# Spreading half of a block-diagonal table on the chip instead of loading it, with a new order of all work

## The chip, the cores and the metric

The kernel runs on one core of a Trainium2 chip. A core has five engines that run side by side, each with its own queue of instructions, worked off in order: PE (matrix products), DVE (vector work), ACT (activations, also copies with a scale), POOL (small vector work) and SP (here only issues DMAs). They meet through semaphores. On-chip data lies in SBUF (128 partitions) and, for PE's results, in eight banks of PSUM. The metric is the device time of one execution in microseconds.

## The reference

Two mixers, A and B, are applied twice in turn to x, of 2048 rows by 512 columns, each on a layer norm and with a residual:

```
x = A_q
x = x + A(layernorm(x));  x = x + B(layernorm(x))
x = x + A(layernorm(x));  x = x + B(layernorm(x))

A: k_shift = sum over 4 taps of shifted k * shift_k;   kv = k_shift * v
   y = irfft(rfft(kv, 4096) * rfft(ssm_k, 4096))[:2048]      (a causal long convolution per column)
   A = q * (y + kv * ssm_D)
B: gelu(layernorm(x) @ w1 + b1) @ w2 + b2                    (512 -> 1376 -> 512)
```

The convolution y does not depend on x, so it is computed once and used by both A layers. Its Fourier transforms are done as matrix products in two stages.

## The kernel before

All data lies in one SBUF tensor, `ar`, cut into named regions. The sequence is worked in two halves of 1024 positions. For the first half the steps are these; the names in brackets are used in the prediction, with the line that the profile gives.

- Loads, all issued by SP in 256 KB pieces: h (`ssm_k`, 4 pieces of a half: h0 to h3), k (k0 to k3), v (v0 to v3), and the second-stage table in 16 pieces (s0 to s15).
- T0 to T3: PE turns a block of h (L540), and DVE or ACT copies it from PSUM as 16-bit values (L473 on ACT, L474 on DVE).
- H1.0 to H1.7: first stage of the transform of h, 16 matmuls each (L557), evicted as 128x1024 (L473 or L474).
- H2.0 to H2.7: second stage (L569), 16 matmuls each. H2.t uses pieces 2t and 2t+1 of the table and all of H1. Eviction as before.
- swap: eight SBUF-to-SBUF DMAs that exchange even and odd partitions of H2's result. The first four need H2.0 to H2.3, the others H2.4 to H2.7.
- K0 to K3: PE turns a quarter of k (L589) and a copy follows. taps: PE turns the filter taps (L520), POOL forms diagonal tap matrices (L527). F0 to F3: the shift filter of a quarter as matmuls (L614). The v products: DVE multiplies a filter's PSUM result with v (L620). Each needs all four pieces of v.
- X1.0 to X1.7 and X2.0 to X2.7: the two stages for kv, with the same table (L557, L569).
- P0.0 to P7.1: sixteen products of the two spectra on DVE (L468, 128x1024). They need X2, H2 and the swapped H2.
- U0 to U3 and G1.0 to G1.7: turn and first stage for the second half of h.
- I1.0 to I1.7 (L674) and I2 (L696): the two stages back. I1.0 to I1.3 need all P with second index 0, the others all P.

Then come the layers: blocks of 128 to 512 rows; for a block statistics on DVE (L810, L811) and POOL (L815, L817, L825), normalisation on DVE (L836) or ACT (L835), product with y and residual (L468), a second statistics and normalisation, a turn (PE, L887, or a DMA), m1 (L899) with gelu on ACT (L904), m2 (L933) with the residual on DVE (L937). The second half's convolution is woven between the blocks.

The order is written out as three constant lists: `SEQ` lists the operations' numbers in the order in which they go to the queues, `ENGS` chooses the engine (a ACT, v DVE, p POOL) for each operation that may run on several, and `BANKS` gives the first PSUM bank of each PSUM tile. `arrange()` reads these, and `sync()` puts in the waits that data and banks demand. The durations in the code are the planner's; nothing waits by them.

The second-stage table holds, for each of 128 small matrices (128 columns each), a weight of 128 x 128 that is zero except where the partition's remainder by 8 equals the group of 16 columns: 7 of 8 values are zero. It is 4 MB in HBM, loaded whole.

Of the kernel before, what the change touches and what calls it, by code (L numbers as in the profile page):

```python
# [7 lines left out]
ALU = mybir.AluOpType  # L8
# [28 lines left out]
class Prog:  # L37
# [65 lines left out]
            "aavvvvvaavvvvvvv")  # L103
    BANKS = (
            "45704306202464200000627236026646246464226006402420624644066042640262264600644466440666002624266260062444"
            "46206466216237643301320727321504123101100322332716373063445423545175402012133355426403067156573421254373"
            "47061653171314250227620662421047670120016563423216502311505064403200454166210125364")

    def __init__(self, nc):
# [283 lines left out]
def bass_interleave_layers__ssm_conv_h3__mixer_channel_mlp__prompt_kernel(  # L393
        nc, A_q, A_k, A_v, A_shift_k, A_ssm_k, A_ssm_D, B_x, B_w1, B_b1, B_w2, B_b2, out):
    P = Prog(nc)
    ar = nc.alloc_sbuf_tensor("ar", [128, AR], BF16)
    NS = 352
# [576 lines left out]
```

## Time and profile before

| | us |
|---|---|
| median of 3 runs | 237.92 |
| lowest, highest | 237.78, 238.18 |
| the profiled execution | 237.62 |
| its span | 235.8 |

| engine | busy us | share of the span |
|---|---|---|
| PE matmul | 223.4 | 95% |
| PE weight load | 146.6 | 62% |
| DVE | 177.0 | 75% |
| ACT | 161.7 | 69% |
| POOL | 55.2 | 23% |

The profile is one execution. Its span goes from the first to the last instruction; 1.8 us of the execution's time lie around it. The shares are means over stages that differ much: the DMA engines move 304 GB/s from 5 to 10 us and 393 GB/s from 15 to 20 us, and 2 GB/s from 90 to 100 us. In the timelines a row that stands for several instructions has their count behind an x; in brackets stands how long the engine had been idle before it and what ended that.

### The profile page before, as it was taken

Reading aid. Unit: us, or ns where it says so; the run is one execution under the profiler, and the core shown is the slowest. Engines: PE = TensorE matmul, PEld = TensorE weight load, DVE = VectorE, ACT = ScalarE, POOL = GpSimd, SP = SyncE. Lnnn points to the kernel's source line nnn. Section 1 sums busy time; section 2 is a strip of 40 time slices with the busy share of each in tenths; the row PEclk is TensorE's granted clock in tenths of the full one; section 3 lists DMA queues with packets and bytes.
Section 4 is the critical chain, followed back from the end, with each engine's and each line's share of the span. In section 5 each row is a group of like instructions: output and inputs, shape, how many; then the busy total and the mean of one; then the engine's idle time right before and its main releaser. Section 6 shows DMA issues by size and latency. Waiting matters only on the chain.

```text
span 235.8 us, 6520 instructions
## 1 busy us (share of the span) xinstructions
PE 223.4 (95%) x2765; PEld 146.6 (62%) x2765; DVE 177.0 (75%) x355; ACT 161.7 (69%) x259; POOL 55.2 (23%) x117
## 2 busy tenths in 40 slices
PE   6796887998999999999999999999999999999995
PEld 3785777875968588667967585644444444444453
DVE  0678989999999999989999899385379388705004
ACT  2962999998996789998987995998037403810910
POOL 1550020924222405344002831402020301100000
PEclk9999999999999999999999999999999999999999
DMA  6999879983976930022140203301300140071302
GB/s 210 301 375 386 311 208 282 264 288 70 174 119 177 198 79 0 3 48 45 31 151 6 45 3 69 67 0 22 67 0 4 22 111 0 0 134 47 133 0 92
DMA packets 41113, 26.77 MB, mean 114 GB/s; under 512 B 23702, under 2 KB 33788, under 8 KB 41084
## 3 DMA queue, kind: packets, MB, share of 16 engines
q1 hardware_dynamic: 40786, 26.20, 41.2%
q8 instruction: 22, 0.36, 0.7%
q10 hardware_dynamic: 298, 0.16, 0.3%
q14 instruction: 7, 0.06, 0.1%
HBM read 15.07 MB, written 2.10 MB: 73 GB/s over the span
## 4 chain that ended last, share of the span: by engine, by line
PE 77%; DVE 7%; ACT 6%; SPq 4%; DMA 4%; issue 1%; DVEq 0%
PE ps L899 33%; PE ps L933 32%; ACT ar L473 6%; PE ps L569 4%; DMA ar<-in_A_v_dram 4%; DVE ar L468 4%; SPq L453 3%; PE ps L674 2%; PE ps L696 2%; DVE ar L620 2%; PE ps L557 2%; DVE ar L474 2%; PE ps L922 1%; PE ps L642 1%; SPq L463 0%
## 5 line engine op out<-in xcount | busy, mean ns | idle before, releaser
L904 ACT ACTIVATE ar<-ps,sm 128x256 bf16<-128x256 f32 (+4 forms) x143 | 64.8, 525 | 35.1 <-PE ps L899 34.8
L473 ACT ACTIVATE ar<-ps 128x1024 bf16<-128x1024 f32 (+3 forms) x77 | 71.6, 1003 | 14.7 <-PE ps L557 6.2
L899 PE MATMUL ps<-ar 128*128 128x256 bf16 (+4 forms) x572 | 81.0, 297 | 0.2 <-ACT ar L473 0.2
L933 PE MATMUL ps<-ar 128*128 128x512 bf16 (+1 forms) x341 | 78.3, 379 | 0.0
L899 PEld LDWEIGHTS ps<-ar 128*128 128x128 bf16 (+1 forms) x572 | 52.7, 100 | 26.1 <-ACT ar L473 0.3
L468 DVE TENSOR_TENSOR ar<-ar 128x512 bf16<-128x512 bf16 (+3 forms) x105 | 62.6, 641 | 4.5 <-ACT ar L473 3.0
L933 PEld LDWEIGHTS ps<-ar 128*128 128x128 bf16 (+1 forms) x341 | 32.5, 98 | 36.5 <-ACT ar L904 0.4
L810 DVE BATCH_NORM_STATS2 sm<-ar 128x6 f32<-128x512 bf16 x64 | 42.6, 682 | 0.4
L835 ACT ACTIVATE ar<-ar,sm 128x512 bf16<-128x512 bf16 x38 | 30.2, 823 | 12.6 <-DVE sm L822 10.5
L815 POOL TENSOR_SCALAR sm<-sm 128x2 f32<-128x2 f32 (+2 forms) x22 | 7.6, 347 | 109.0 <-DVE sm L811 108.4
L937 DVE TENSOR_TENSOR ar<-ar,ps 128x512 bf16<-128x512 bf16 x31 | 20.4, 679 | 16.1 <-PE ps L933 16.1
L817 POOL TENSOR_TENSOR sm<-sm 128x2 f32<-128x2 f32 (+2 forms) x26 | 21.2, 814 | 21.8 <-DVE sm L815 19.9
L557 PE MATMUL ps<-ar 128*64 128x128 bf16 x512 | 17.2, 221 | 2.8 <-POOL ar L468 1.2
L569 PE MATMUL ps<-ar 128*128 128x64 bf16 x512 | 18.3, 193 | 1.3 <-ACT ar L473 0.9
L569 PEld LDWEIGHTS ps<-ar 128*128 128x128 bf16 x512 | 16.9, 98 | 3.2 <-ACT ar L473 1.4
L557 PEld LDWEIGHTS ps<-ar 128*64 128x64 bf16 x512 | 14.8, 110 | 5.6 <-ACT ar L473 1.6
L474 DVE CAST ar<-ps 128x1024 bf16<-128x1024 f32 x13 | 15.8, 1220 | 2.4 <-PE ps L569 1.3
L836 DVE TENSOR_SCALAR ar<-ar,sm 128x512 bf16<-128x512 bf16 x26 | 9.9, 406 | 5.1 <-POOL sm L825 5.0
L825 POOL TENSOR_SCALAR sm<-sm 128x1 f32<-128x1 f32 x40 | 13.2, 347 | 1.9
L674 PE MATMUL ps<-ar 64*128 64x64 bf16 (+1 forms) x384 | 12.6, 203 | 0.5 <-ACT ar L473 0.3
L674 PEld LDWEIGHTS ps<-ar 64*128 64x128 bf16 (+1 forms) x384 | 11.9, 114 | 1.9 <-ACT ar L473 1.2
L767 DVE SCALAR_TENSOR_TENSOR ar<-ar,sm,ps 128x512 bf16<-128x512 bf16 x16 | 10.9, 744 | 0.4 <-PE ps L569 0.4
(42 smaller groups left out, 90.3 us busy)
## 6 DMA issues: line engine op xcount, KB each, us to landing
ar<-tab_s SPq DMA_DIRECT2D x16, 256.0 KB, 9.0
ar<-ar SPq DMA_DIRECT2D x16, 256.0 KB, 4.5
ar<-in_A_ssm_k_dram SPq DMA_DIRECT2D x8, 256.0 KB, 7.1
ar<-in_A_q_dram SPq DMA_DIRECT2D x8, 256.0 KB, 4.9
ar<-in_A_v_dram SPq DMA_DIRECT2D x8, 256.0 KB, 6.8
out_dram<-ar SPq DMA_DIRECT2D x7, 256.0 KB, 2.5
ar<-in_B_w_dram SPq DMA_DIRECT2D x4, 344.0 KB, 5.6
ar<-in_B_w_dram SPq DMA_DIRECT2D x5, 256.0 KB, 4.1
```

The costliest lines, as they stand in the source:

```text
L468: return P.op(eng, lambda e: e.tensor_tensor(o, a, b, op), dur, reads=[a, b] + list(more), writes=[o])
L473: return e.activation(dst, src(), AF.Copy)
L474: return e.tensor_copy(dst, src())
L557: r = e.matmul(Q(tl, 64 * ri, 64, i * 128, [1, 128]), w, m, start=True, stop=True)
L569: r = e.matmul(Q(tl, 0, 128, i // 8 * 512 + i % 8 * 4, [32, 16], [1, 4]), w, m, start=True, stop=True)
L674: r = e.matmul(Q(tl, 0, 128, i, *([32, 16], [1, 4]) if split else ([1, 128],)), w, m, start=n == 0, stop=n == 1)
L810: P.op(DVE, lambda e, sj=sj, x=x: e.bn_stats(sj, x), 600.0, reads=[x], writes=[sj])
L817: P.op(POOL, lambda e: e.tensor_tensor(r, v, hf, ALU.pow), 420.0 + 149.0 * n, reads=[v, hf], writes=[r])
L835: return e.activation(o, x, AF.Identity, bias=u, scale=r)
L899: r = e.matmul(Q(tl, 0, rows, 0, [1, w]), a, m, start=dk == 0, stop=dk == 3)
L904: P.op(ACT, lambda e, dst=dst, tl=tl, rows=rows, bias=bias, w=w: e.activation(dst, Q(tl, 0, rows, 0, [1, w]), AF.Gelu_apprx_tanh, bias=bia ...
L933: r = e.matmul(Q(tl, 0, 128, 0, [1, 512]), ins[fc][0], ins[fc][1], start=fc == 0, stop=fc == 10)
```

## The change

The table in HBM has two parts now: C, 128 x 2048, with the values and no zeros, and the whole one behind it. Of C the first 1024 columns are loaded into the region of w1 (`R_C`, 256 KB), which stands for the first half of the whole table. The second half, pieces s8 to s15, is loaded whole as before. Pieces s0 to s7 are not loaded. In their place eight operations "spread" (SP0 to SP7) write the first half: SPd copies all 64 groups of 16 values of C to column group d of 64 matrices, multiplied per partition with a mask that is 1 where the partition's remainder by 8 is d, and 0 elsewhere. So each writes 128 x 1024 values in runs of 16, and each of H2.0 to H2.3 and X2.0 to X2.3 needs all eight. On DVE a spread is a `tensor_scalar`, on ACT an activation with a scale. One small copy makes the masks (on POOL, after the small table's load).

All three lists of the order are new. What stands where on the queues for the first part, in the order of the queue (loads of 256 KB unless marked; other small work left out or named by its kind):

```
SP before:  h2 h0 h1 h3 q0 k1 k3 k2 k0 q1 v2 q2 v0 (bias) v1 s12 s4 v3 s3 (small) s7 s6 s1 s5 s8 s13 s2 s0 hh1
            s11 s10 hh3 s15 s9 s14 hh2 hh0 | swaps 0 1 2 3 4 5 7 6 | rest of q, w1, w2, T2
SP after:   h3 h1 h0 k3 k0 k1 k2 C h2 q0 v2 v3 v1 v0 s11 s8 s15 hh2 q3 hh3 s14 (small) q1 (bias) hh0 s9 s13 s10
            w1 q2 s12 hh1 (bias) | swaps 0 1 3 2, one piece of w2, swaps 5 4 6 7 | rest of w1, w2, T2
DVE before: taps d0 T3 2 statistics H1.3 . . H1.6 . H1.2 K0 K2 K1 . V3 V1 V2 V0 X1.2 3 statistics X1.5 H2.1 X1.0
            statistic . X1.3 . H2.7 . X2.1 U3 P1.0 P0.0 U0 P2.0 P3.0 P0.1 P7.0 P6.0 P4.0 P5.0 P5.1 P6.1 P3.1 P7.1
            P2.1 P4.1 P1.1
DVE after:  T1 T0 H1.3 K1 SP0 SP4 taps 2 statistics K2 SP2 K3 . . V2 SP5 V0 . V1 SP3 V3 SP6 X1.0 . statistic X1.3 . .
            X1.4 statistic . . H2.1 statistic U0 . H2.7 statistic H2.4 P0.0 P3.0 X2.2 U3 P1.1 P2.0 P2.1 P1.0 P6.0
            P4.0 P5.0 P7.0 P7.1 P0.1 P6.1 P5.1 P3.1 P4.1
ACT after:  loads, T3 H1.7 H1.6 H1.0 H1.1 K0 SP1 T2 H1.2 H1.5 H1.4 SP7 (norm) X1.2 U2 H2.3 H2.2 X1.6 H2.0 X1.1 X1.7
            X1.5 H2.5 X2.3 X2.0 H2.6 X2.6 X2.1 G1.1 X2.4 X2.7 X2.5 ...
PE after:   warm T3 T1 T0 H1.7 H1.3 H1.6 H1.0 H1.1 K1 K0 H1.2 taps T2 K2 K3 F0 F2 H1.5 H1.4 F1 F3 X1.0 X1.2 U2 X1.6
            H2.3 H2.2 X1.3 X1.4 H2.0 X1.1 X1.7 H2.1 X1.5 U0 H2.5 H2.7 X2.3 X2.0 H2.4 H2.6 ...
```

(V0 to V3 are the v products, hh the second half of h, d0 an addition of one row, a point a small operation of up to 0.2 us.) In the new order H1.4 uses the PSUM banks of V2's filter, so its matmuls wait on PE for V2. The normalisation ahead of the first block's turn is on ACT before and on DVE after. The shift taps' load stands behind ACT's table load instead of ahead of it.

The diff, with the number lists cut:

```diff
     SEQ = (
-        42, 0, 6, 43, 214, 1, 4, 33, 2, 5, 34, 41, 7, 3, 195, 9, 11, 10, 8, 196, 51, 14, 197, 45, 52, 12, 209, 46, 35,
...
+        0, 46, 8, 45, 35, 2, 6, 3, 5, 36, 12, 9, 1, 10, 11, 25, 4, 44, 217, 7, 56, 197, 15, 50, 16, 57, 14, 13, 47,
...
     ENGS = (
-            "avapapvpaavvaavaavaaaaavvvvapvppvavvavaavaavvaaaaaaaavaaaaaaaaavaavaaaaaapvpvaaaaaaaaaaaaaaaaaaaaaaaaaaa"
...
+            "pvavvvvvavpvpapapaaavaaaaavaavaavavavvvppvvvaavvaaavaavvaaaaaaaaavaaaaavaaaavaaaaaaapppvaaaaaaaaaaaaaaaaaa"
...
     BANKS = (
-            "45704306202464200000627236026646246464226006402420624644066042640262264600644466440666002624266260062444"
...
+            "26624320240260660466027405640260464422140204626240406006442460424046462002242440224402622420604066466004"
...
@@ -358,13 +358,18 @@
-    S2 = np.zeros((2, 8, 8, 128, 2, 8, 8))
-    for d in range(8):
-        S2[0, :, d, :, 0, :, d] = c
-        S2[1, :, d, :, 0, :, d] = s
-        S2[0, :, d, :, 1, :, d] = -s
-        S2[1, :, d, :, 1, :, d] = c
-    S2 = S2.transpose(0, 1, 2, 3, 6, 5, 4).reshape(128, 128 * 128)
+    S2 = np.zeros((2, 8, 8, 128, 8, 2))
+    S2[0, :, :, :, :, 0] = c[:, None]
+    S2[1, :, :, :, :, 0] = s[:, None]
+    S2[0, :, :, :, :, 1] = -s[:, None]
+    S2[1, :, :, :, :, 1] = c[:, None]
+    C2 = S2.reshape(128, 2048)
+    S2 = np.zeros((128, 128, 8, 16))
+    pd = list(range(8))
+    for j in range(8):
+        m = np.arange(128) % 8 == pd[j]
+        S2[m, :, j] = C2.reshape(128, 128, 16)[m]
+    S2 = np.concatenate([C2, S2.reshape(128, 16384)], 1)
@@ -383,6 +388,7 @@
     sg = np.where(np.arange(128)[:, None] % 2 == 0, -1.0, 1.0) * np.ones((1, 16))
+    sg[:, 8:] = np.arange(128)[:, None] % 8 == np.arange(8)
@@ -441,9 +447,10 @@
+    R_C = R_W1
-    M_B1, M_ST, M_MV, M_RS, M_HF, M_NM, M_SG = 0, 16, 208, 240, 256, 260, 276
-    assert M_SG + 1 <= NS
+    M_B1, M_ST, M_MV, M_RS, M_HF, M_NM, M_SG, M_MK = 0, 16, 208, 240, 256, 260, 276, 284
+    assert M_MK + 8 <= NS
@@ -494,11 +501,25 @@
+    tload(t_s2, 18432, 0, R_C, 1024)
     load_h(0, R_1)
     load_t(A_k, 0, R_8, 2)
     load_t(A_v, 0, R_8 + 4096, 2)
-    for i in range(16):
-        tload(t_s2, 128 * 128, i * 1024, R_S2 + i * 1024, 1024)
+    for i in range(8, 16):
+        tload(t_s2, 18432, 2048 + i * 1024, R_S2 + i * 1024, 1024)
+    P.tag = "spread"
+    mk, src = M(0, 128, M_MK, [1, 8]), A(0, 128, R_SG + 8, [1, 8])
+    P.op((DVE, POOL), lambda e, mk=mk, src=src: e.tensor_copy(mk, src), {DVE: 65.0, POOL: 190.0}, reads=[src], writes=[mk])
+    for h in range(1):
+        for d in range(8):
+            o, c, m = A(0, 128, R_S2 + 8192 * h + 16 * d, [128, 64], [1, 16]), A(0, 128, R_C + 1024 * h, [16, 64], [1, 16]), M(0, 128, M_MK + d, [1, 1])
+
+            def f(e, o=o, c=c, m=m):
+                if e is nc.scalar:
+                    return e.activation(o, c, AF.Copy, scale=m)
+                return e.tensor_scalar(o, c, m, None, ALU.mult)
+            P.op(BOTH, f, {ACT: 912.0, DVE: 395.0}, reads=[c, m], writes=[o])
+    P.tag = ""
     tload(t_sm, row, 464, R_U, 256)
```

More of the change, by code (lines that the diff above doesn't have):

```diff
@@ L44 @@
     SEQ = (
[55 rows of a table removed]
[55 rows of a table added]
     ENGS = (
-            "avapapvpaavvaavaavaaaaavvvvapvppvavvavaavaavvaaaaaaaavaaaaaaaaavaavaaaaaapvpvaaaaaaaaaaaaaaaaaaaaaaaaaaa"
-            "aappappaavpvppaappvvppaapvaappaappaapvaappaappavppvappaappaappvvppaappvappaaavvvvvaappvaaapvvvavpvvvavpp"
-            "aavvvvvaavvvvvvv")
+            "pvavvvvvavpvpapapaaavaaaaavaavaavavvvppvvvaavvaaavaavvaaaaaaaaavaaaaavaaaavaaaaaaapppvaaaaaaaaaaaaaaaaaa"
+            "aaaaaaaaaaapvapvvavpvppaappvvppaavpaappaappaappaappaappaappavppaappaavpvvppavppaapvaavavvvaaapvvavvvpaav"
+            "vpvvvvavvavvvvvavavpvvvaa")
     BANKS = (
-            "45704306202464200000627236026646246464226006402420624644066042640262264600644466440666002624266260062444"
-            "46206466216237643301320727321504123101100322332716373063445423545175402012133355426403067156573421254373"
-            "47061653171314250227620662421047670120016563423216502311505064403200454166210125364")
+            "26624320240260660466027405640260464422140204626240406006442460424046462002242440224402622420604066466004"
+            "64437020665061071760610567714342477554774645676076415011601640607710627426534031026021423236345773476356"
+            "05721367332244501304047053300705405345357130760457666515312732321600130735714203533")
     def __init__(self, nc):
```

108 rows, old and new, of the table SEQ are left out of this document.

## The prediction

> **What bounds the kernel now.** I read the page first, then busy time by stretches of the span, then the chain that ended last, then the timelines of DVE, ACT and SP over the first 60 us. Times below are microseconds from the span's start. The first fence has the page's lines of the span and of the engines, and then the stretches (per engine: busy time and instructions; then the clock, DMA share and GB/s).
>
> ```profile
> span 235.8 us, 6520 instructions
> ```
>
> ```profile
> 0.00:42.66 42.66, 34.02 (x787) 28.92 (x788) 30.80 (x45) 30.65 (x33) 10.06 (x31) 1.00 0.91 294
> 42.66:58.02 15.36, 14.37 (x240) 11.53 (x241) 14.49 (x32) 14.66 (x17) 7.29 (x11) 1.00 0.74 213
> 58.02:235.80 177.78, 175.06 (x1738) 106.17 (x1738) 131.68 (x280) 116.40 (x210) 37.87 (x77) 1.00 0.28 62
> ```
>
> From 58.02 on PE is idle for 2.7 us of 177.8, and most of that is the tail after its last matmul. There an earlier arrival of anything wins nothing; the end is where PE's saturated stretch begins, plus its work. What can be won lies before 58: 8.6 us of idle PE up to 42.66 and 1.0 after it. The chain says what holds PE there (start, length, what):
>
> ```profile
> 4.57 1.21 SPq L453
> ...
> 10.05 8.55 DMA ar<-in_A_v_dram
> ...
> 23.47 0.65 PE ps L569 x16
> ...
> 40.45 6.12 DVE ar L468 x10
> ...
> 57.28 0.70 ACT ar L835
> 58.02 0.41 PE ps L887 x4
> 59.11 0.84 PE ps L899 x12
> ...
> 233.45 0.29 DVE ar L926
> ```
>
> The last load of v, issued at 10.05, lands at 18.60; the four v products follow on DVE, then evictions and the spectrum products until 46.57 (40.45 + 6.12). The DVE timeline gives the durations (start, length, group; idle before it in brackets):
>
> ```profile
> 18.68 4.74 DVE L620 TENSOR_TENSOR ar<-ps,ar 128x1024 bf16<-128x1024 f32 x4 [2.09 <-DMA ar<-in_A_v_dram]
> 23.33 1.22 DVE L474 CAST ar<-ps 128x1024 bf16<-128x1024 f32 x1
> 24.46 1.87 DVE L810 BATCH_NORM_STATS2 sm<-ar 128x6 f32<-128x512 bf16 x3
> 27.75 2.36 DVE L474 CAST ar<-ps 128x1024 bf16<-128x1024 f32 x2 [0.29 <-PE ps L569]
> 32.55 1.23 DVE L474 CAST ar<-ps 128x1024 bf16<-128x1024 f32 x1 [0.39 <-PE ps L569]
> 34.51 1.23 DVE L474 CAST ar<-ps 128x1024 bf16<-128x1024 f32 x1 [0.66 <-PE ps L569]
> 35.65 0.68 DVE L474 COPY ar<-ps 128x1024 bf16<-128x1024 bf16 x1
> 38.05 8.51 DVE L468 TENSOR_TENSOR ar<-ar 128x1024 bf16<-128x1024 bf16 x14
> ```
>
> Neighbours overlap a little, so by steps a v product is 1.18, an eviction 1.16, a statistic 0.62, a 16-bit copy from PSUM 0.60 and a spectrum product 0.61. DVE's idle in this stretch is 0.29 + 0.39 + 0.66 = 1.34 us: from 18.68 on, DVE is the bound, and ACT beside it nearly so. What v's lateness costs is 2.09 us of idle DVE.
>
> **The loads.** Seven loads of 256 KB fewer go out, and the order on SP changes: the last load of v is the 14th large load instead of the 17th, the small table C the 8th. The SP timeline, with the landings of the same loads (us from issue) after it:
>
> ```profile
> 8.51 0.36 SPq L453 DMA_DIRECT2D ar<-in_A_v_dram  x1
> 10.05 0.50 SPq L453 DMA_DIRECT2D ar<-in_A_v_dram  x1
> 29.76 2.52 SPq L453 DMA_DIRECT2D ar<-ar  x2
> ```
>
> ```profile
> ar<-in_A_k_dram SPq DMA_DIRECT2D x2, 256.0 KB, 6.8
> ar<-in_A_v_dram SPq DMA_DIRECT2D x1, 256.0 KB, 8.1
> ar<-in_A_v_dram SPq DMA_DIRECT2D x1, 256.0 KB, 8.5
> ar<-ar SPq DMA_DIRECT2D x2, 256.0 KB, 4.7
> ```
>
> The 14th large load landed at 8.51 + 8.1 = 16.6, the 17th at 18.6. v is complete at 16.6, 2.0 us earlier. k moves up to the 4th to 7th place, h's block 2 down to the 9th; the 9th was issued at 4.57 and landed 6.8 later, at 11.4, the 8th a little before, so C is there near 11 (estimate from these rows). The table's whole half is spread over the 15th to 31st places, between q and the second half of h; its first user in stage 2 comes after H2.1's eviction (29.5, below), and an equal place landed several us before that, so it costs nothing; were that cover gone, PE would wait load by load, 0.65 us each (2.0 / 3). The loads of W1, W2 and the biases that now stand before or among the swaps have users from 59.11 on; one load of W2 between the swaps delays the later swaps by one issue, whose first product, P6.0, stands seventh. shift_k's load goes behind ACT's table load, while its user, the taps, moves back on PE behind K0 and H1.2.
>
> **The spreads.** No spread is in the trace. The nearest rows (line, operation, forms, count, busy, mean ns):
>
> ```profile
> L836 DVE TENSOR_SCALAR ar<-ar,sm 128x512 bf16<-128x512 bf16 x3 | 1.2, 402 | 0.0
> L468 DVE TENSOR_TENSOR ar<-ar 128x1024 bf16<-128x1024 bf16 x16 | 9.8, 691 | 0.0
> L811 DVE BATCH_NORM_AGGREGATE sm<-sm 128x2 f32<-128x6 f32 x10 | 1.4, 167 | 0.0
> L473 ACT ACTIVATE ar<-ps 128x1024 bf16<-128x1024 f32 x38 | 36.3, 1045 | 7.0 <-PE ps L557 5.9 <-PE ps L674 0.5 <-PE ps L569 0.3
> ```
>
> The same operation on half the elements is 0.40 (0.33 as a step, less the 0.07 to 0.08 by which neighbours overlap (0.691 against 0.61)), so that is the lower end; a product of two tensors of the same size is 0.69 (0.61 as a step), the upper. The operation is L836's, so I lean to it: 0.47, the middle of the steps, six times on DVE. On ACT a spread is at most the 1.0 of an eviction. [...]
>
> Spreads 0, 4 and 2 lie on DVE before the first v product. From C's arrival and the K1 copy before them, 11.6 (11 + 0.6), stand three spreads (1.41), the taps' copy (0.2), two statistics (1.24), two copies (1.20) and two small ones (0.34): done by 16.0, before v's 16.6, so they cost nothing; the cover is 0.6 us. The two on ACT fall into this row's gap:
>
> ```profile
> 21.62 1.02 ACT L473 ACTIVATE ar<-ps 128x1024 bf16<-128x1024 f32 x1 [4.79 <-PE ps L557]
> ```
>
> Spreads 5, 3 and 6 stand between the v products, on the path. Before, products to first eviction took 23.33 - 18.68 = 4.65. Now it is 4.65 + 3 x 0.47 + 0.15 for a small operation moved in from POOL = 6.2, so from 16.65 the first X1 eviction starts at 22.85: of 2.0 us, 0.5 is left. H2.3, the first second-stage group, needs all eight spreads and starts near 22.9 to 23.1, against 23.47. PE's queue has one new tie: H1.4 waits for the bank that the first v product frees (17.8), and filter F1 stands behind it; a stage group and a filter need some 1.6 us, and DVE comes to F1's product at 19.6, so it costs nothing with 0.2 to spare.
>
> **From there to the end of the spectrum products.** Both orders hold seven evictions, four statistics, two copies and sixteen products on DVE; the new one holds 0.48 more of small ones (a halo copy, an aggregate, a two-scalar step). Before: 46.57 - 23.33 = 23.24, less its 1.34 of waits, 21.9; after 22.4, to 45.2 without waits. But the swap loads wait for H2.1's eviction, which DVE now ends at 22.85 + 4 x 1.16 + 2 x 0.62 + 0.81 = 29.5, against 28.9 (27.75 + 1.16). The second swap moves from 29.76 to 30.4 and lands 4.7 later, at 35.1. The first product P0.0 could go at 45.2 - 16 x 0.61 - 1.16 - 0.60 = 33.7. It waits 1.4 us, everything behind it on DVE as well, and the products end at 46.6, against 46.57: zero. So the load that was late is paid back, and the next late thing is the swap. Bounds: -1.4 if the swaps land earlier on the emptier queue, +0.7 if spreads take 0.69.
>
> **The hand-over to the block.** Before, ACT evicts until 57.28, then normalises (0.70), PE turns (0.41), ACT copies, and the first m1 matmul is at 59.11. The new order puts that normalisation on DVE. DVE reaches it near 56.7 by its list (statistics and products of the first block from 52.8, then POOL's two steps, 0.9 together), so ACT no longer stands in line. This takes up to 0.7 from the chain. PE's idle there, 0.99, is the most that can go. I take -0.6; bounds 0 and -1.0.
>
> **The saturated stretch and the tail.** A fresh order cannot win there (2.7 us idle, of it 235.8 - 233.45 = 2.35 behind the last matmul) and can open new holes: 0 to +1.2, about as many as the stretch before 58 has. I take +0.2. The last four matmul groups are reordered, with the same pieces: zero. ACT, with as many evictions in both orders, gains what DVE gains.
>
> **Sum.** 0 - 0.6 + 0.2 = -0.4. The profiled execution took 237.62 us, so 237.2; the median of the runs is 0.30 above it, which gives 237.5.
>
> [...] POOL's two copies under DVE's run of products show a lock; the second line is the same size of copy when DVE was on other work (min/median/max ns):
>
> ```profile
> L632 POOL COPY ar<-ar x2: 199/2638/5077, 41.5 to 46.7; 128x3 bf16<-128x3 bf16 x2
> ```
>
> ```profile
> L603 POOL COPY ar<-ar x3: 189/190/191, 15.0 to 16.1; 128x3 bf16<-128x3 bf16 x3
> ```
>
> One copy took 5.08 us instead of 0.19. [...]
>
> **Rivals.**
> Slow spreads (slower): place, between the v products; price, 0.69 each and a wait on POOL, so the first X1 eviction at 23.5 to 24, the swaps at 30.3 to 30.7, and the products' end 0.7 to 1.3 later: 238.2 to 238.8. For it: it stores runs of 16 elements, a shape that no TENSOR_SCALAR row has. Against it: L836. It decides from 0.64 us a spread, where 3 x 0.17 eats the 0.5 that is left. Chance 0.28; the lock is 0.08 of it.
> The new order leaves holes in the saturated stretch (slower): 1.0 to 2.0 above the sum, 238.5 to 239.5. For it: nothing there can improve. Against it: PE's queue there holds blocks with two engines at 75% or less. Chance 0.14.
> The gain passes through (faster): spreads at 0.33 and no wait for the swaps, -0.4 - 1.4 on top of the sum: 235.7; half of it, 236.6. For it: seven loads less are queued ahead of the swaps. Against it: the swaps stood behind the last of the other loads before, too. Chance 0.20.
> My forecast, 237.0 to 238.0: chance 0.38.
>
> **How the numbers follow.** A run of this kernel tells 0.2% (0.48 us) from no change: faster is under 237.44, slower over 238.40. The forecast's 0.38 splits 0.20 faster, 0.18 same; the passing gain is faster, 0.20; slow spreads 0.03 same and 0.25 slower; holes 0.14 slower. Together 0.40, 0.21, 0.39. The range goes from half to nearly all of the passing gain, 235.9, to the worst of the holes, 239.5. The likeliest case alone has 237.0 to 238.0.
>
> **What would show it.** DVE's bracket before L620 gone or small, with its first row near 16.6; three TENSOR_SCALAR of 128x1024 between L620 rows, of 0.4 to 0.55; the first L569 near 23; the swaps' first issue near 29.6, and DVE idle before L468 with a DMA as releaser; the last L468 near 46.6; L835 gone from the chain at 57. Wrong it would be if L620 began before 16 or after 17.5, if L468 did not wait, or if PE idled more than 3.5 us behind 58.

## The result

| | before | changed |
|---|---|---|
| median us | 237.78 (22 runs) | 236.59 (22 runs) |
| lowest, highest | 237.21, 240.32 | 235.99, 240.65 |
| ratio, 95% interval | | 0.9955 [0.9935, 0.9975] |
| the profiled execution's span | 235.8 | 237.0 |

The change wins 0.45%. In two later comparisons the same kernel gave 0.9988 [0.9958, 1.0019] and 0.9941 [0.991, 0.9971], so the gain lies between nothing and 0.6%, most likely near 0.4%. Executions of the changed kernel are spread more than its gain is wide, and the profiled one is 2.2 us above its median (238.78). In some comparisons a part of the executions had a mean granted clock of 0.993 or less and was some 1.6 us longer (6 of 35 of the kernel before beside e9 to e12, with a median of 239.5 against 237.9; 4 of 12 in e5; 7 of 10 in e3; none of 12 in e9), so medians of different comparisons differ by that as well. So the traces below are read for mechanisms, and the sizes are compared over several of them.

The profile of the changed kernel. First the page's line of the span, then the busy time in the stretches used before (columns as before):

```profile
span 237.0 us, 6515 instructions
```

```profile
0.00:42.66 42.66, 35.65 (x814) 30.00 (x815) 33.27 (x54) 35.05 (x38) 11.27 (x34) 1.00 0.86 274
42.66:58.02 15.36, 14.76 (x252) 11.92 (x250) 14.96 (x33) 14.49 (x21) 3.78 (x9) 1.00 0.67 167
58.02:237.00 178.98, 173.74 (x1710) 104.10 (x1706) 130.84 (x278) 116.26 (x208) 34.91 (x68) 1.00 0.26 60
```

Up to 58 us PE did 2.0 us more work than before (35.65 + 14.76 against 34.02 + 14.37). Behind 58 it is idle for 5.2 us of its span, against 2.7 before: the front got faster, and the saturated stretch got holes. The DVE timeline shows the front:

```profile
13.79 0.68 DVE L520 TENSOR_SCALAR ar<-ar,sm 128x1024 bf16<-128x1024 bf16 x1
15.33 1.23 DVE L641 TENSOR_TENSOR ar<-ps,ar 128x1024 bf16<-128x1024 f32 x1
16.47 0.48 DVE L520 TENSOR_SCALAR ar<-ar,sm 128x1024 bf16<-128x1024 bf16 x1
16.86 1.22 DVE L641 TENSOR_TENSOR ar<-ps,ar 128x1024 bf16<-128x1024 f32 x1
21.34 1.22 DVE L481 CAST ar<-ps 128x1024 bf16<-128x1024 f32 x1
32.81 1.28 DVE L475 TENSOR_TENSOR ar<-ar 128x1024 bf16<-128x1024 bf16 x2
36.20 8.52 DVE L475 TENSOR_TENSOR ar<-ar 128x1024 bf16<-128x1024 bf16 x14 [0.37 <-issue]
```

The first v product (now L641) starts at 15.33 with no wait; before, L620 waited until 18.68. Spreads are L520. The first X1 eviction is at 21.34 (23.33 before), and the products end at 36.20 + 8.52 = 44.72 (46.57). The loads behind this, in the SP timeline and the times to landing (the last load of v, the second swap):

```profile
7.72 0.46 SPq L460 DMA_DIRECT2D ar<-in_A_v_dram  x1
...
28.77 2.77 SPq L460 DMA_DIRECT2D ar<-ar  x4
```

```profile
ar<-in_A_v_dram SPq DMA_DIRECT2D x1, 256.0 KB, 7.3
ar<-ar SPq DMA_DIRECT2D x1, 256.0 KB, 2.9
```

v is complete at 7.72 + 7.3 = 15.0. The second swap, issued at 29.52, lands at 32.4, ahead of the first product. The chain that ended last, from the hand-over on, and PE's two waits on it:

```profile
55.21 0.41 PE ps L908 x4
...
56.30 0.84 PE ps L920 x12
...
66.84 4.29 DMA ar<-ar
71.19 4.55 PE ps L920 x40
...
79.31 4.88 DMA ar<-ar
84.25 7.60 PE ps L920 x68
```

```profile
71.19 4.98 PE L920 MATMUL ps<-ar 128*128 128x256 bf16 x44 [1.06 <-DMA ar<-ar]
84.25 5.96 PE L920 MATMUL ps<-ar 128*128 128x256 bf16 x53 [1.61 <-DMA ar<-ar]
```

The normalisation on ACT is gone from the hand-over, and the first m1 matmul is at 56.30 instead of 59.11. But PE then waits 1.06 and 1.61 us for the DMA transposes (L900) that bring the normalised rows of blocks 2 and 3 to m1. Before, m1 had no such wait:

```profile
72.29 4.98 PE L899 MATMUL ps<-ar 128*128 128x256 bf16 x44
83.58 9.33 PE L899 MATMUL ps<-ar 128*128 128x256 bf16 x84
```

That is the second half of the story: 2.7 us which the prediction had as 0.2.

### The profile page after: what moved, and what is told of

Read it like the earlier page. It is cut to its first block, busy times and chain, and to the rows that moved or that the text cites. A ratio compares the mean times of both kernels' runs of the same rounds, so it can differ in the third digit from the quotient of the medians.

```text
span 237.0 us, 6515 instructions
## 1 busy us (share of the span) xinstructions
PE 224.1 (95%) x2765; PEld 146.0 (62%) x2765; DVE 179.1 (76%) x363; ACT 165.8 (70%) x263; POOL 50.0 (21%) x110
## 4 chain that ended last, share of the span: by engine, by line
PE 75%; ACT 8%; DMA 8%; DVE 5%; SPq 1%; issue 1%
PE ps L920 32%; PE ps L954 28%; DMA ar<-ar 6%; ACT ar L480 6%; PE ps L695 4%; PE ps L590 3%; PE ps L578 3%; DMA ar<-in_A_ssm_k_dram 2%; ACT ar L856 2%; DVE ar L475 2%; DVE ar L641 2%; PE ps L717 1%; DVE ar L481 1%; PE ps L635 1%; SPq L460 1%
## 5 line engine op out<-in xcount | busy, mean ns | idle before, releaser
L925 ACT ACTIVATE ar<-ps,sm 128x256 bf16<-128x256 f32 (+4 forms) x143 | 66.1, 521 | 37.2 <-PE ps L920 36.8
L954 PE MATMUL ps<-ar 128*128 128x512 bf16 (+1 forms) x341 | 79.6, 379 | 0.0
L475 DVE TENSOR_TENSOR ar<-ar 128x512 bf16<-128x512 bf16 (+2 forms) x104 | 62.9, 642 | 5.9 <-ACT ar L856 4.4
L954 PEld LDWEIGHTS ps<-ar 128*128 128x128 bf16 (+1 forms) x341 | 32.3, 98 | 35.1 <-ACT ar L925 0.2
L856 ACT ACTIVATE ar<-ar,sm 128x512 bf16<-128x512 bf16 x39 | 30.7, 811 | 10.2 <-DVE sm L843 10.2
L838 POOL TENSOR_TENSOR sm<-sm 128x2 f32<-128x2 f32 (+2 forms) x26 | 21.4, 824 | 41.4 <-DVE sm L836 39.8
L836 POOL TENSOR_SCALAR sm<-sm 128x2 f32<-128x2 f32 (+2 forms) x19 | 5.9, 310 | 92.0 <-DVE sm L832 91.8
L578 PE MATMUL ps<-ar 128*64 128x128 bf16 x512 | 18.3, 221 | 1.9 <-ACT ar L480 1.2
L481 DVE CAST ar<-ps 128x1024 bf16<-128x1024 f32 x11 | 13.4, 1216 | 1.5 <-PE ps L578 1.2
L832 DVE BATCH_NORM_AGGREGATE sm<-sm 128x2 f32<-128x6 f32 x64 | 10.5, 173 | 0.8
```

What stands on the lines that cost most here:

```text
L475: return P.op(eng, lambda e: e.tensor_tensor(o, a, b, op), dur, reads=[a, b] + list(more), writes=[o])
L578: r = e.matmul(Q(tl, 64 * ri, 64, i * 128, [1, 128]), w, m, start=True, stop=True)
L838: P.op(POOL, lambda e: e.tensor_tensor(r, v, hf, ALU.pow), 420.0 + 149.0 * n, reads=[v, hf], writes=[r])
L856: return e.activation(o, x, AF.Identity, bias=u, scale=r)
L925: P.op(ACT, lambda e, dst=dst, tl=tl, rows=rows, bias=bias, w=w: e.activation(dst, Q(tl, 0, rows, 0, [1, w]), AF.Gelu_apprx_tanh, bias=bia ...
L954: r = e.matmul(Q(tl, 0, 128, 0, [1, 512]), ins[fc][0], ins[fc][1], start=fc == 0, stop=fc == 10)
```

## The experiments

The theories. **A, the place:** v's place in the queue of loads sets the front; the smaller table and the spreads are not what wins. **B, the bytes:** the front wins because seven loads of 256 KB less go out. **C, swap traffic:** the waits near 71 and 84 come from the second half's swaps on the same DMAs. **D, instruction packets,** formed after C fell: a 16 KB packet of the queue that loads instructions holds one DMA engine while a transfer needs a part from that engine. Several edits move operations in `SEQ` with this helper:

```diff
+def _put(seq, ids, after):
+    s = [i for i in seq if i not in ids]
+    k = s.index(after) + 1
+    return tuple(s[:k]) + tuple(ids) + tuple(s[k:])
```

All runs in one table. "Products" is the end of the last spectrum product, "m1" the start of the first m1 matmul, "rest" the span less that, "wait" what PE then waits for DMA transposes behind m1; all four come from the one profiled execution. Ratios are medians against the kernel before on the same chip.

| kernel | median us | ratio, 95% | products | m1 | rest | wait |
|---|---|---|---|---|---|---|
| before | 237.78 | 1 | 46.57 | 59.11 | 176.7 | 0 |
| changed | 236.59 | 0.9955 [0.9935, 0.9975] | 44.72 | 56.30 | 180.7 | 2.67 |
| e5 changed, again | 237.52 | 0.9988 [0.9958, 1.0019] | 44.88 | 56.46 | 178.7 | 0.91 |
| e9 changed, again | 236.55 | 0.9941 [0.991, 0.9971] | 46.39 | 57.98 | 177.6 | 0 |
| e1 before, v early (with q) | 245.42 | 1.0322 [1.0287, 1.0358] | 54.49 | 67.05 | 176.7 | 0 |
| e12 before, v early, q0 kept | 236.85 | 0.9944 [0.992, 0.9969] | 45.82 | 58.36 | 176.7 | 0 |
| e2 changed, table loaded whole | 241.59 | 1.016 [1.0123, 1.0196] | 48.50 | 60.08 | 178.7 | 0.97 |
| e3 changed, v late | 239.38 | 1.0069 [1.0039, 1.0099] | 45.99 | 57.58 | 179.0 | 1.20 |
| e4 changed, three spreads twice | 237.26 | 0.9984 [0.9958, 1.0009] | 46.38 | 57.96 | 177.6 | 0 |
| e6 changed, swaps split | 237.72 | 0.9998 [0.998, 1.0016] | 45.32 | 56.91 | 179.6 | 1.64 |
| e7 changed, without second swaps | 236.79 | 0.9962 [0.9939, 0.9986] | 45.45 | 57.03 | 178.9 | 1.11 |
| e8 changed, norm on ACT | 238.18 | 1.0007 [0.9989, 1.0025] | 45.37 | 57.64 | 179.0 | 1.05 |
| e10 changed, 56 warm-ups | 237.31 | 0.9959 [0.9932, 0.9986] | 46.26 | 57.84 | 177.7 | 0 |
| e11 changed, 92 warm-ups | 237.86 | 0.9994 [0.9967, 1.0021] | 45.42 | 57.00 | 178.0 | 0.21 |

**e1: v early in the order of before.** v's four loads go ahead of three q loads and two table pieces.

```diff
+    SEQ = _put(SEQ, (14, 12, 13, 15, 28, 20, 195, 196, 197), after=8)
```

> The kernel before, with whole table and its own order; on SP the four loads of v go ahead of three loads of q and two pieces of the table (v is complete with the 12th large load instead of the 17th), nothing else moves. Theory A (what held the front was v's place in the load queue, and the spreads only buy that place): the first v product starts near 16.5 instead of 18.68, limited by the filters on PE, the first m1 matmul comes 1 to 2 us before 59.11, and the time falls by 0.5 to 1.5 us, much as with the whole change. Theory B (the table's bytes were the limit, the place of v alone does nothing because the second stage then waits for its pieces): v products start as early, but the first second-stage group stays near 23.5, and the time moves by less than 0.3 us.

It took 3.2% more, for a reason of its own. One of the loads moved back is q0, and early statistics on it (L818) stand in DVE's queue ahead of the copies of k. The chain, and then the stretches from 10 to 25 us (columns as before):

```profile
8.73 8.55 DMA ar<-in_A_q_dram
```

```profile
10.00:15.00 5.00, 0.69 (x18) 0.48 (x16) 0.00 (x0) 1.61 (x2) 1.68 (x4) 1.00 1.05 377
15.00:20.00 5.00, 0.23 (x6) 0.24 (x8) 2.70 (x6) 0.00 (x0) 0.04 (x1) 0.58 1.06 391
20.00:25.00 5.00, 4.75 (x84) 4.29 (x82) 3.34 (x5) 2.38 (x3) 2.52 (x7) 0.74 1.05 387
```

DVE stood until 17.3, PE starved behind it (0.23 us busy of the 5 from 15 to 20) and its granted clock was 0.58 in these 5 us. The run says nothing for A or B: the edit made another load the late one. e12 mends that.

**e12: the same with q0 left in its early place.** No C, no spreads, the same bytes as before.

```diff
+    SEQ = _put(SEQ, (14, 12, 13, 15, 28, 20, 196, 197), after=8)
```

> The kernel before with v's four loads ahead of two table pieces and of q1 and q2, with q0 left in its early place: no C, no spreads, the same bytes. If v's place in the queue alone holds the front: v near 16.6, first v product near 16.7, first X1 eviction near 21.4 (no spreads on the path), products end 1 to 2 us earlier, time 0.3 to 0.8% under before. If the whole table's bytes are needed in time: a DMA of the table or of q ends a wait on DVE or PE between 17 and 27, the first m1 matmul stays at 59 or later, and the time is that of before or up to 1% above.

The SP timeline, the landing of the third and fourth of v's loads, the DVE timeline and the chain:

```profile
5.92 2.19 SPq L461 DMA_DIRECT2D ar<-in_A_v_dram  x4
```

```profile
ar<-in_A_v_dram SPq DMA_DIRECT2D x2, 256.0 KB, 7.3
```

```profile
17.24 4.73 DVE L628 TENSOR_TENSOR ar<-ps,ar 128x1024 bf16<-128x1024 f32 x4 [0.82 <-PE ps L622]
21.89 1.21 DVE L482 CAST ar<-ps 128x1024 bf16<-128x1024 f32 x1
...
37.30 8.52 DVE L476 TENSOR_TENSOR ar<-ar 128x1024 bf16<-128x1024 bf16 x14
```

```profile
58.36 0.85 PE ps L907 x12
```

v is no longer what the first product waits for; the filter on PE (L622) is, and the product starts at 17.24 instead of 18.68. The first X1 eviction follows 1.44 us earlier than before, the products end 0.75 earlier, m1 starts 0.75 earlier. The time is 0.9944 [0.992, 0.9969], beside 0.9941 [0.991, 0.9971] for the changed kernel on the same chip. One line that moves loads gives as much as the whole change. That decides for A in this sense: v's place alone is worth as much, and the seven loads did not have to go for it. In the one profile 0.75 us of the 1.2 in the median are seen, all of them in the front (the rest behind m1 is 176.7 in both). That the change itself wins by v's place and not in another way is argued from the front, where its first X1 eviction (21.34, in e5 21.81, in e9 21.96) comes near e12's 21.89.

**e3: the changed kernel with v late,** its last load the 17th large one again.

```diff
+    SEQ = _put(SEQ, (15, 16, 14, 13), after=24)
```

> The changed kernel with the four v loads put behind three pieces of the table (17th large load again instead of the 14th). Theory A: the first v product starts near 17.0 to 17.5 instead of 15.33, the first m1 matmul comes 1.5 to 2 us later than 56.30, and the time is 1 to 2 us above the changed kernel's. Rival (the holes of PE behind 60 us swallow it: waits there shrink by what the front loses): the first m1 matmul is as late, but the time rises by less than 0.5 us.

```profile
16.76 1.23 DVE L649 TENSOR_TENSOR ar<-ps,ar 128x1024 bf16<-128x1024 f32 x1 [0.97 <-DMA ar<-in_A_v_dram]
...
39.88 6.11 DVE L483 TENSOR_TENSOR ar<-ar 128x1024 bf16<-128x1024 bf16 x10 [0.54 <-DMA ar<-ar]
```

The wait for v is back (0.97), the products end 1.1 to 1.3 us later than in the changed kernel's first two profiles, and the median is 1.9 to 2.8 us above the changed kernel's. With the spreads kept and v late the kernel is 0.7% slower than before. The sign is that of A, but the profile doesn't carry the size: the products end at 45.99, earlier than in e9 (46.39), where v is early, and m1 starts 1.5 us ahead of the kernel before. What this execution lost against before lies behind m1 (179.0 against 176.7), 1.20 us of it in the wait near 71; why the median is higher still was not traced.

**e2: the changed kernel with the table loaded whole,** without C and spreads: eight whole loads for s0 to s7 behind v, the planner's list otherwise kept.

```diff
-    tload(t_s2, 18432, 0, R_C, 1024)
...
-    for h in range(1):
-        for d in range(8):
...
+    for o, n in ((7, 2), (4, 2), (5, 2), (0, 2), (1, 2), (2, 2), (3, 1), (3.5, 1)):
+        tload(t_s2, 18432, 2048 + int(o * 1024), R_S2 + int(o * 1024), 512 * n)
...
+    SEQ = _put(SEQ, (137, 4, 26, 27, 28, 29, 30, 31, 32, 33), after=13)
+    ENGS = ENGS[0] + ENGS[9:]
```

> The changed kernel in its new order without C and without the spreads: the first half of the table is loaded in eight loads again, behind v and the first of the second h loads; all later loads move back by some five us of DMA time. Theory A: v at the same time as in the changed kernel, DVE free of six spreads and ACT of two, so the first part is as fast or faster (first eviction of X1 up to 1.2 us earlier), and the time within 0.5 us of the changed kernel's 236.6. Theory B: the pieces behind (s8 to s15) now come too late, PE waits for a DMA at the second-stage groups that use them, and the time is 1 to 2 us above the changed kernel's.

```profile
25.73 0.69 DVE L833 BATCH_NORM_STATS2 sm<-ar 128x6 f32<-128x512 bf16 x1 [3.75 <-DMA ar<-in_A_q_dram]
```

It lost 1.6%, but up to there nothing waits for the table, and the front is no slower without the spreads (first X1 eviction at 20.69 instead of 21.34). Then DVE waited 3.75 us for a q load that the table had pushed back, and m1 starts 3.8 us later than in the changed kernel. So the change's order does need the table to be short, because its list puts q's statistics early. Read together with e12: the bytes matter only through what an order puts behind them.

**e4: spreads 5, 3 and 6 done twice,** the second time into a free region, so 1.2 us more on DVE between the v products.

```diff
+                if o2 is not None:
+                    e.tensor_scalar(o2, c, m, None, ALU.mult)
                 return e.tensor_scalar(o, c, m, None, ALU.mult)
...
+            o2 = A(0, 128, R_5 + 16 * d, [128, 64], [1, 16]) if d in (5, 3, 6) else None
```

> The changed kernel with spreads 5, 3 and 6 done twice, the second time into a region that is free then: three more tensor_scalar of 128x1024 between the v products, 0.40 us each by steps. If DVE's queue is what sets the front (theory A and the prediction), the first eviction of X1 comes 1.2 us later than 21.34, the spectrum products end 0.8 to 1.2 later than 44.72, and the time rises by 0.5 to 1.2 us. If ACT or a DMA sets it, the end of the spectrum products moves by less than 0.4.

The first X1 eviction starts 1.3 us later than in e5 (23.15 against 21.81), the products end at 46.38 and m1 starts at 57.96, both 1.5 us later. The rise of the time that was expected did not come: the median is that of e5 (0.9984 against 0.9988). In this profile the wait near 71 is gone (rest 177.6), which pointed at that wait. The two profiles alone don't prove it, for e9 below ends its products as late with nothing added.

**e5: the changed kernel again,** the measure for e6 to e8.

> The changed kernel as it is, for a second profile of it, since the first profiled execution (238.78) lies 2.2 us above its median. Theory C (in the stretch behind 60 us, DMA transposes of the normalised tiles share the DMA engines with the eight swap loads of the second half, and how late they land differs from run to run): in an execution near 236.5 the two waits of PE for a DMA there (1.06 and 1.61 us in the first profile) are smaller by 1.5 us or more together, and the front up to the first m1 matmul (56.3) is the same within 0.3. Rival (the slow execution was slow in its front or its clock): the first m1 matmul differs by a us or more.

```profile
36.36 8.52 DVE L475 TENSOR_TENSOR ar<-ar 128x1024 bf16<-128x1024 bf16 x14 [0.38 <-issue]
```

```profile
71.19 4.98 PE L920 MATMUL ps<-ar 128*128 128x256 bf16 x44 [0.91 <-DMA ar<-ar]
```

The wait near 71 is there again, the one near 84 is not, and m1 starts at 56.46. That is what C had expected; e7 is the test that decides on it.

**e6: four of the second half's swaps behind the transposes of block 3. e7: all eight left out** (the second half's convolution is then formed without the exchanged partitions).

```diff
+    SEQ = _put(SEQ, (271, 268, 269, 270), after=497)
+    SEQ = _put(SEQ, (273, 274, 272, 275), after=551)
```

```diff
-    swap(R_3, R_HS1)
...
+    SEQ = tuple(i if i < 268 else i - 8 for i in SEQ if not 268 <= i < 276)
```

> The changed kernel with the eight second-half swaps parted on SP: the four that the first two products of that half need stay, the other four go behind the next block's two transposes (z3). Theory C: the z3 transposes land nearer to 2.5 us than to 4.9 us after issue, PE's wait before that block's m1 shrinks, and the time falls by 0.3 to 1.0 us below the changed kernel's. Rival (the wait there comes from the late normalisation on ACT, not from the DMA engines): within 0.3 us of the changed kernel; or slower, if the products of that half then wait for the last four swaps.

> The changed kernel without the eight second-half swaps (the second half's spectrum is left without its exchanged part, so the output is not the reference's): takes their traffic away. Theory C: the z2 transposes land about 2.5 us after issue, no PE wait for a DMA above 0.5 us between 60 and 90 us, few slow executions, and the time 1 to 2.5 us below the changed kernel's. Rival (transposes are slow by themselves): they land as late as with the swaps, and the time is within 0.3 us.

e6 won nothing (0.9998 against 0.9988): its waits are 1.22 and 0.42. e7 kept the wait though nothing else was moving; its median is 0.7 us below e5's and not the 1 to 2.5 that C had expected. Its stretches, the DMA queues from 69.4 to 71.9, and PE:

```profile
69.70:70.00 0.30, 0.30 (x40) 0.29 (x28) 0.30 (x2) 0.00 (x0) 0.00 (x0) 1.00 0.00 0
70.00:71.90 1.90, 0.69 (x18) 0.21 (x3) 1.90 (x6) 0.00 (x0) 0.00 (x0) 1.00 0.00 0
```

```profile
q8 instruction: 1, 0.02, 3.0%
```

```profile
71.96 4.21 PE L921 MATMUL ps<-ar 128*128 128x256 bf16 x37 [1.11 <-DMA ar<-ar]
```

From 69.7 to 71.9 no transfer moved on the DMA engines (last two columns: share 0.00, 0 GB/s), and still the transpose had not landed. C falls as the cause of this wait. The only other thing in that time is one packet of the instruction queue. The trace's single packets and completions tell more. Each of these transfers has 16 completions in the trace, and the page gives the time of the DMA queues as a share of 16 engines, so I take a completion for the end of one engine's part:

```
kernel, transfer               15th part   last part   instruction packet (start, us)
changed, block 2, 2nd tile       69.35       71.14       68.93, 1.14
changed, block 3, 2nd tile       82.10       84.20       82.14, 0.88
e5, block 2                      69.50       71.15       69.13, 0.95
e6, block 2                      69.95       71.90       69.59, 1.20
e7, block 2                      70.08       71.92       69.66, 1.21
e8, block 2                      70.69       72.47       70.13, 1.23
e3, block 2                      70.62       72.56       70.54, 0.95
e4, block 2                      71.01       71.02       70.87, 1.26
e9, block 2                      71.02       71.03       71.57, 0.95
before, block 2                  69.81       69.82       71.58, 0.93
```

In each wait (the first seven rows), 15 of the 16 parts were done 1.6 to 2.1 us ahead of the last, and a 16 KB instruction packet was under way as the 15th part ended, or started 0.04 us behind that (second row). Where the packet came behind or nearly behind the transfer (the last three rows), all parts ended together and PE did not wait. In e7 the trace shows the delay itself: the last two packets of the transfer, of 4 bytes each, start at 70.85 and 70.86, just as the instruction packet ends (69.66 + 1.21 = 70.87).

These rows are a choice. The 14 traces hold 529 transposing transfers in all. In 312 of them no instruction packet (of 16 or 8 KB) was under way from the issue to 0.06 us behind the 15th part, and in none of these did the last part come more than 0.1 us behind the 15th. In the other 217 it came 0.9 to 2.1 us behind in 25, and by at most 0.7 in the rest. So a late part always had a packet beside it, but a packet beside a transfer mostly cost no part of its own: on which engine a packet lay, the traces don't say. PE waited for nine of the 25. The kernel before has three of them (issued at 81.61, 102.51 and 205.46) and waits for none.

The page of the changed kernel counts 22 such packets of 16 KB; PE's 5530 instructions by 22 are 251 for each, 65 bytes an instruction. That they are PE's own code is my estimate from this count; no trace says whose code a packet holds. (In e11 there are also 22 for 5700 instructions, 259 for each, so their number doesn't follow the instructions exactly.)

**e8: the norm ahead of the first turn back on ACT** (one letter of `ENGS`).

> The changed kernel with the one normalisation ahead of the first turn moved back from DVE to ACT, at the same place of the order. By the prediction's term for the hand-over: the first m1 matmul comes 0.5 to 0.8 us later than 56.30, and PE's idle before it grows by as much. If the saturated stretch behind it swallows that in its own waits, the time rises by less than 0.3 us; otherwise by 0.4 to 0.8.

From the end of the products to the first m1 the changed kernel takes 11.58 or 11.59 us in every one of its profiles; e8 takes 57.64 - 45.37 = 12.27. So this edit is worth 0.69 us at its place. The median is 0.66 above e5's (238.18 against 237.52), inside the 0.4 to 0.8 that was expected.

**e9 to e11: moving the packets.** e9 is the changed kernel, e10 and e11 put more, shorter warm-up matmuls at the start, where PE works on zeros while it waits for the first loads. If the packets are PE's code, all later ones then go out some instructions earlier.

```diff
-        for i in range(7):
-            r = e.matmul(Q(tl, 0, 128, 0, [1, 512]), z[:, :128], z, start=True, stop=True)
+        for i in range(56):
+            r = e.matmul(Q(tl, 0, 128, 0, [1, 64]), z[:, :128], z[:, :64], start=True, stop=True)
```

(e11: 92 of 32 columns.)

> The changed kernel once more, as the measure for the three beside it. Code-load theory: near 68 to 70 us one 16 KB packet of the queue that brings instructions lies on one DMA engine for 0.9 to 1.2 us, the second transposing transfer of block 2 has 15 of its 16 parts done some 1.8 us before the last, and PE stands 0.9 to 1.2 us near 71 for it. The time is 236.5 to 237.7.

> The changed kernel, with the 7 warm-up matmuls of 512 columns at the start replaced by 56 of 64 columns: 98 instructions more on PE (matmuls and weight loads), about the same 3.2 us of work on zeros, before any load has landed. Code-load theory: PE's instructions come in packets of 16 KB, so all later packets go out 98 instructions earlier, the one near 69 by about 2 us (some 47 instructions a us there), before the second transposing transfer of block 2 has its data; the wait near 71 us falls from about 1.0 to under 0.3, and the time is 0.2% to 0.5% under the changed kernel of this call. Rival, that the order alone makes the transfer late (the normalisation before it, or traffic of other loads): the wait stays at 0.9 to 1.2 and the time is the same.

> The same with 92 warm-up matmuls of 32 columns, 170 instructions more. [...] Rival: wait and time unchanged.

e9 missed its expectation: its front was 1.5 us slower than e5's at the same code, and its packet came at 71.57, behind the transfer. What made the front slower is open; it fell behind in steps, 0.15 us by the first X1 eviction (21.96 against 21.81) and 1.2 by the first spectrum product (34.13 against 32.96), and between them PE once stood for 0.81 us, up to 28.93, for nothing that the profile shows. So there was no wait to take away here, and the times can't show a gain. What the three traces do show is that the packets move and the waits with them: the first 16 KB packet starts at 13.16 in e9, 10.66 in e10 and 8.77 in e11. In e11, m1 starts at 57.00, as in e7 (57.03, wait 1.11). Its transposes, the queues from 70.8 to 72.5, where its packet now is, and PE:

```profile
ar<-ar SPq DMA_TRANSPOSE x2, 2.5
```

```profile
q8 instruction: 1, 0.02, 3.4%
```

```profile
70.66 4.97 PE L920 MATMUL ps<-ar 128*128 128x256 bf16 x44
```

Both transposes land in 2.5 us, all parts of the second by 70.06, the packet starts at 71.55, and PE has no wait near 71. Another packet, at 80.09, now meets a transfer of block 3 (15th part 80.73, last 82.27), and PE waits 0.21 us for it. In e10 a packet fell somewhere else. The DVE timeline, the landing of the second swap, and the queues from 32.3 to 34.8:

```profile
34.80 1.29 DVE L475 TENSOR_TENSOR ar<-ar 128x1024 bf16<-128x1024 bf16 x2 [1.50 <-DMA ar<-ar]
```

```profile
ar<-ar SPq DMA_DIRECT2D x1, 256.0 KB, 4.9
```

```profile
q8 instruction: 1, 0.02, 2.4%
```

Here 15 parts of the second swap were done by 32.81 and the last at 34.78, with the packet from 32.76 to 33.73. DVE waited 1.50 us in front of the first product, and the products ended at 46.26. This supports D by two traces, each of one execution; no run here ties a packet to a median. As a remedy the padding failed: 237.31 and 237.86 against 236.55 for e9. Why e11's median is 1.3 us above e9's, while its profiled span is 0.6 us shorter, stays open.

## Why the prediction came out as it did

The time, 236.59, lies inside the range 235.9 to 239.5 and on the predicted side, 0.9 us under the point of 237.5 and outside the likeliest case's own 237.0 to 238.0. It is at the upper end of the rival in which the gain passes through (235.7 to 236.6, chance 0.20). All three signs that I had named for being wrong came: the v products before 16, no wait for the swaps, and more than 3.5 us of idle PE behind 58. The time fell into the range because their errors had opposite signs, which is luck.

**v's arrival: right mechanism, 1.6 us too late.** I took the old landing of the 14th large load, 16.6. It came at 15.0, for its issue moved up as well: 7.72 instead of 8.51, and 7.3 instead of 8.1 us to landing. The first product started at 15.33, not near 16.65.

**The spreads: right in kind, 0.07 too long.** The six on DVE take 0.51 us in the mean and 0.48 where undisturbed, with steps of 0.39 to 0.40 between the v products; I had 0.47 a step. The rows, from the groups of instructions:

```profile
L520 DVE TENSOR_SCALAR ar<-ar,sm 128x1024 bf16<-128x1024 bf16 x6 | 3.0, 512 | 0.0
L519 ACT ACTIVATE ar<-ar,sm 128x1024 bf16<-128x1024 bf16 x2 | 2.3, 1164 | 0.0
```

On ACT a spread took 1.16, above the 1.0 that I had called the most; it was hidden, for ACT's last one ended near 19.4 and DVE's last at 21.42. The rival of slow spreads falls. Of the lock that I had put there, the runs show one slower spread, ahead of v's first product: the spread at 13.79 took 0.68 while POOL formed taps (L548) until 14.19, and in e11, with POOL done at 14.48, the same spread, at 14.51, took 0.48. No run shows the waits on POOL that carried the rival up to 238.8: the three spreads between the v products took 0.48 each, the one at 16.47 beside POOL's L838 (16.54 to 17.36). Nor do the rows show more of a lock than one copy: in the kernel before, the copy of 5.08 us ran from 41.54 to 46.61, as DVE's products ended (46.57), and the other, at 46.74, stood behind them; in the changed kernel the copy at 38.87 (L653) took 0.48 beside the same products (36.20 to 44.72). From first product to first X1 eviction took 6.01 (21.34 - 15.33; I had 6.2).

**The swaps: the step that failed.** I had the second swap land 4.7 us after its issue, and 1.4 us of waiting for it, so that the front's gain came to zero. It landed in 2.9 and nothing waited: the products ended at 44.72, 1.85 earlier. The bound of -1.4 was for this case. But the row of 4.7 was no property of a queue's length, as I had it. In e10 the swap took 4.9, and the wait was 1.50; what differed was an instruction packet that ran as its 15th part ended. In before, the second swap's 15th part ended at 32.88 and its last at 34.37, so 1.5 us of that row's 4.7 were one late part too, with a packet from 30.31 to 31.84. Over its profiles the changed kernel's products end between 44.72 and 46.39.

**The hand-over: right in size, paid elsewhere.** I had -0.6; e8 measures 0.69 for that edit. From products to m1 it is 11.58 instead of 12.54. But the rest behind m1 is 177.6 to 177.7 us even in the profiles with no wait (e4, e9, e10), against 176.7 before: 0.9 more stands behind m1. One second-stage group is part of it (208 of these matmuls behind m1 instead of 192, some 0.47 us); what the other half is was not traced. So the net of the two is about zero, which I had not looked for.

**The saturated stretch: the term that was mis-sized.** I had +0.2, at most +1.2. The profiled execution had 2.67 us of waits for transposes, e5 0.91, e9 none. The rival of holes (1.0 to 2.0) had the right place with no mechanism; the mechanism that the traces point to is that of the packets. Against e9, the transfer of block 2 that was late starts 1.5 to 1.7 us earlier (67.00 in e5 and 66.84, against 68.52), and the packet 2.4 to 2.6 us earlier (69.13 and 68.93, against 71.57), so that it meets the transfer. So of 1.85 us won at the products, the profiled execution gave back all and more, e5 two thirds (its span is 0.6 us shorter than before's), and the median kept 1.2.

## What to carry to other kernels

Before shrinking a load, try the same bytes in another order: here one line that moved v ahead of two table pieces and two q loads was worth as much as the half table, the spreads and a whole new order. A load that is moved back must be followed to its first user on every queue (e1 and e2 each lost over 1.5% to a q load whose statistics stood early on DVE). A transfer that lands late on idle DMA engines should be looked at part by part, and an order searched to within 1 us should leave slack ahead of any transfer that PE waits for; here up to 2 us were needed.

## What the runs showed of the hardware

- In seven transposes and one swap that PE or DVE waited for, the last of 16 parts came 1.6 to 2.1 us behind the 15th, beside a 16 KB instruction packet of 0.88 to 1.23 us. Of 312 transposes without a packet beside them none had a part over 0.1 us late. The profile names the wait after the transfer, and in e7 the DMA share shows 0.00 meanwhile.
- With a code-only shift (98 or 170 more instructions of warm-up on PE) the packets came earlier and such a wait stood at another transfer (e10 and e11, one profile of each).
- The same kernel's front differed by up to 1.7 us between profiles (products' end 44.72, 44.88, 46.39), and its times by 2.4 us within one comparison (235.62 to 238.01, e9), more than the change's gain.
- In e1 PE was busy for 0.92 us from 10 to 20. Its granted clock was 1.00 in the first five of these and 0.58 in the second, and 0.74 in the next five, though PE was then busy for 4.75 of 5.
